# A two-layer decode step: late loads of round two split anew, a maximum in halves, variance, ReLU and outputs moved

## Chip, cores and metric

The kernel runs on one core of a Trainium2 chip. The metric is the device time of one execution in microseconds (us); of several runs the median counts.

## The reference

Four tokens (batch 4, width 640) pass through attention, an MLP, attention again and the MLP again, with the same weights and the same caches in both rounds. All data are float32.

```python
x = x + A(layernorm(x), k_cache, v_cache, wq, wo)   # 32 heads of 128; the last 1024 cache rows
x = x + B(layernorm(x), w1, w2)                     # relu(x @ w1) @ w2, hidden width 1728
x = x + A(layernorm(x), k_cache, v_cache, wq, wo)
x = x + B(layernorm(x), w1, w2)
```

In `A`, q = x @ wq, then for each batch and head softmax(q k^T / sqrt(128)) over 1024 positions, times v, then all heads @ wo. `layernorm` has no gain or bias.

## The kernel before

**Data.** Each head is one record `rec` of 9472 float32 columns on 128 partitions (4736 KB): 640 columns of wq, 4096 of keys (`K`), 4096 of values (`V`), 640 of wo (`WO`). The MLP weights `wm` are 17280 columns. A `store` in SBUF holds five records and the first `FIRST` = 2176 columns of head 0; `ring` (4320 columns) takes MLP weights and parts of records, `kept` (2688) the end of head 26.

**Loads.** All loads stand in one list, `items`, in a fixed order, and are issued by SP in that order. `pump()` issues the next one as soon as no live columns overlap its place; `done(key, lo, hi)` frees columns after the instructions that read them and calls `pump()`. So a load waits for the last reader of its place, and all loads behind it wait too. A semaphore makes SP wait on the chip for that reader.

**Order of heads.** Round one takes heads 0 to 31, round two 27 to 31 and then 0 to 26 (`order`). Heads 27 to 31 are still in the store from round one and are not loaded again, nor are the first 2176 columns of head 0 and the end of head 26. While heads 27 to 31 are computed in round two, what they leave is filled with heads 1 to 5, piece by piece: `places` lists free stretches of the store in the order of use, `run` cuts the stream of records to them at the columns of `CUTS`. `old[i]` is the place of the i-th of the heads 27 to 31. Part of head 31 is parked in PSUM (`park`, copied back by `unpark`) so that MLP weights have room in the place called `spare`.

**One head.** `query`: wq times x (10 matmuls), scaled by VectorE into `qT`. `scores`: 16 matmuls into one of two PSUM tiles `sc_ps` (128 x 1024). `softmax`: maximum on VectorE, exp on ScalarE. `weights`: transpose in 32 x 32 blocks on VectorE and scaling. `values`: 16 matmuls into `o_ps`. `picks`: mask and reduction on VectorE. `output_T`: a matmul that transposes, copied by ScalarE to `oTs`. `project`: wo, 8 matmuls added into `acc`, which holds x. The scores of the next head are issued ahead of the values of this one.

**Start of a round and MLP.** `center` takes the mean off; `deviation` computes the variance (a matmul by ones into a few columns of `acc`, small VectorE steps, a square root on ScalarE). For attention it stands behind the first half of the first head's scores; the first head's query stays unscaled, and its scores are scaled in the exponential. In `mlp` it stands behind the first of five blocks of w1. Then ReLU with the scale on ScalarE (two activations and a copy of 16 columns), transposes on VectorE into `hT`, and 54 tiles of w2.

**Fillers.** `busy` issues matmuls whose result is not used. Every engine executes its instructions in the order in which they are written (`InOrder`, so that most profile lines name line 102).

## Time and profile before

| | |
|---|---|
| median of 3 runs | 713.27 us (712.83 to 715.55) |
| profiled execution | 714.82 us |
| its span | 713.0 us |
| granted TensorE clock | 0.818 |
| TensorE busy (matmuls) | 496.7 us, 70% of the span |
| VectorE busy | 317.3 us, 45% |
| ScalarE busy | 102.2 us, 14% |
| data moved by DMA | 301.98 MB, mean 424 GB/s |

PE is TensorE's matmuls, PEld its weight loads, DVE VectorE, ACT ScalarE, SPq the queue of SyncE on which the loads are issued. A row of the windows view gives a stretch of the span, its length, for each engine busy time and instructions, then the granted TensorE clock, the busy share of the DMA engines and GB/s. A row of the timeline gives start, duration, engine, source line, operation and tiles; in brackets is the idle time before it and what ended it. In the chain of waits each piece has start, duration, engine and tile. Round one ends and round two begins at about 386 us.

### The profile page before, as it was taken

Reading aid. Unit: us, or ns where it says so; the run is one execution under the profiler, and the core shown is the slowest. Engines: PE = TensorE matmul, PEld = TensorE weight load, DVE = VectorE, ACT = ScalarE, POOL = GpSimd, SP = SyncE. Lnnn points to the kernel's source line nnn. Section 1 sums busy time; section 2 is a strip of 40 time slices with the busy share of each in tenths; the row PEclk is TensorE's granted clock in tenths of the full one; section 3 lists DMA queues with packets and bytes.
Section 4 is the critical chain, followed back from the end, with each engine's and each line's share of the span. In section 5 each row is a group of like instructions: output and inputs, shape, how many; then the busy total and the mean of one; then the engine's idle time right before and its main releaser. Section 6 shows DMA issues by size and latency. Waiting matters only on the chain.

```text
span 713.0 us, 8685 instructions
## 1 busy us (share of the span) xinstructions
PE 496.7 (70%) x3722; PEld 202.1 (28%) x3722; DVE 317.3 (45%) x647; ACT 102.2 (14%) x218; POOL 1.1 (0%) x9
## 2 busy tenths in 40 slices
PE   0685684678577468869868899655584676675986
PEld 0321231232232223333314333221231232223322
DVE  2252362353453353546631866525262353363650
ACT  0110110011010110111221321101010011020210
POOL 0000000000000000000000000000000000000000
PEclk9986797677686776877999999979597688797998
DMA  9999999999999999999999999999999999999995
GB/s 396 438 415 449 434 415 445 445 412 442 448 410 442 444 420 425 422 444 421 422 405 409 410 432 424 428 453 432 420 440 435 430 433 425 440 424 422 431 422 237
DMA packets 12598, 301.98 MB, mean 424 GB/s; under 512 B 1408, under 2 KB 1552, under 8 KB 4624
## 3 DMA queue, kind: packets, MB, share of 16 engines
q1 hardware_dynamic: 12528, 301.42, 98.6%
q8 instruction: 29, 0.48, 0.2%
q14 instruction: 9, 0.07, 0.0%
q10 hardware_dynamic: 32, 0.01, 0.0%
HBM read 301.34 MB, written 0.08 MB: 423 GB/s over the span
## 4 chain that ended last, share of the span: by engine, by line
DMA 74%; PE 20%; DVE 3%; another core or an unknown queue 1%; issue 1%; ACT 1%; SPq 0%; ACTq 0%; DVEq 0%
DMA store<-rec 67%; PE sc_ps L102 7%; PE o_ps L102 6%; DMA store<-wm 4%; PE acc L102 3%; PE misc L102 3%; DMA ring<-wm 3%; DVE scratch L102 1%; DVE o_ps L102 1%; ACT oTs L102 1%; DVE small L102 0%; DVE store L102 0%; ACT sc_ps L102 0%; DVE sc_ps L102 0%
## 5 line engine op out<-in xcount | busy, mean ns | idle before, releaser
L102 PE MATMUL sc_ps<-store,qT 128*4 128x512 f32 x1024 | 184.6, 812 | 40.3 <-DMA store<-rec 38.4
L102 PE MATMUL misc<-xT,store 128*128 128x4 f32 x620 | 95.0, 280 | 103.9 <-DMA store<-rec 103.6
L102 PE MATMUL o_ps<-store,scratch 128*16 128x512 f32 x954 | 144.4, 683 | 3.1 <-DVE scratch L102 1.9
L102 DVE TENSOR_REDUCE small<-sc_ps 128x1 f32<-128x1024 f32 x64 | 78.4, 1225 | 148.3 <-PE sc_ps L102 148.3
L102 PEld LDWEIGHTS misc<-xT,store 128*128 128x128 f32 x620 | 89.5, 225 | 161.2 <-DMA store<-rec 125.4
L102 ACT ACTIVATE sc_ps<-sc_ps,small 128x1024 f32<-128x1024 f32 (+1 forms) x68 | 71.5, 1051 | 328.8 <-DVE small L102 316.4
L102 DVE STREAM_TRANSPOSE sc_ps<-sc_ps 128x1024 f32<-128x1024 f32 (+1 forms) x70 | 81.7, 1167 | 0.1
L102 DVE TENSOR_TENSOR o_ps<-o_ps,of_block 128x512 f32<-128x512 f32 x62 | 43.3, 699 | 51.3 <-PE o_ps L102 46.0
L102 PEld LDWEIGHTS sc_ps<-store,qT 128*4 128x4 f32 x1024 | 31.9, 104 | 120.2 <-issue 62.7
L102 PEld LDWEIGHTS o_ps<-store,scratch 128*16 128x16 f32 x954 | 32.8, 113 | 112.8 <-issue 96.8
L102 DVE TENSOR_TENSOR qT<-misc,rows 128x4 f32<-128x4 f32 x61 | 9.5, 156 | 116.0 <-PE misc L102 116.0
L102 PE MATMUL acc<-store,oTs 128*4 128x160 f32 x488 | 34.1, 362 | 18.1 <-ACT oTs L102 17.3
L102 DVE TENSOR_REDUCE scratch<-o_ps 128x128 f32<-128x512 f32 x62 | 42.9, 691 | 2.1
L102 ACT COPY oTs<-o_ps 128x4 f32<-128x4 f32 x62 | 10.1, 162 | 218.0 <-PE o_ps L102 218.0
L102 PE MATMUL o_ps<-rows,scratch 128*128 128x4 f32 x124 | 26.3, 282 | 13.1 <-DVE scratch L102 13.1
L102 PEld LDWEIGHTS o_ps<-rows,scratch 128*128 128x128 f32 x124 | 22.0, 222 | 20.6 <-DVE scratch L102 16.8
L102 DVE TENSOR_TENSOR scratch<-sc_ps,mrt 128x128 f32<-128x128 f32 (+1 forms) x70 | 19.6, 280 | 3.1 <-PE o_ps L102 0.5
L99 PE MATMUL acc<-scratch,ring 128*128 128x160 f32 x2 | 0.9, 539 | 22.3 <-DMA scratch<-xf 22.3
L102 DVE TENSOR_SCALAR mrt<-of_batch,small 128x4 f32<-128x4 f32 x64 | 14.7, 229 | 2.2
L102 PE MATMUL acc<-kept,small 128*1 128x328 f32 (+1 forms) x44 | 14.8, 448 | 0.0
L102 PEld LDWEIGHTS acc<-store,oTs 128*4 128x4 f32 x488 | 6.8, 84 | 24.3 <-ACT oTs L102 22.2
L102 DVE STREAM_TRANSPOSE scratch<-small 128x32 f32<-128x32 f32 x64 | 12.9, 201 | 1.4 <-ACT sc_ps L102 1.4
(83 smaller groups left out, 128.1 us busy)
## 6 DMA issues: line engine op xcount, KB each, us to landing
store<-rec SPq DMA_DIRECT2D x14, 7872.0 KB, 28.3
store<-rec SPq DMA_DIRECT2D x7, 7936.0 KB, 29.6
store<-rec SPq DMA_DIRECT2D x5, 7104.0 KB, 21.4
store<-rec SPq DMA_DIRECT2D x9, 2368.0 KB, 36.1
store<-rec SPq DMA_DIRECT2D x3, 4736.0 KB
store<-rec SPq DMA_DIRECT2D x2, 4416.0 KB, 29.0
store<-rec SPq DMA_DIRECT2D x5, 1024.0 KB, 18.6
store<-rec SPq DMA_DIRECT2D x2, 2304.0 KB, 15.8
```

The source lines that it names most:

```text
L99: r = build(*args, **kwargs)
L102: r = build(*args, **kwargs)
```

## The change

1. `places`: the entry for the wo columns of head 27 is dropped; the last long stretch ends at `FROM` of the place of head 31; then come the first 2176 columns of the store (head 0's, free in round two behind its first scores), the rest of head 31's place, and the ring. Round one no longer frees head 0's first 2176 columns.
2. `deviation` moves from behind the first half of the first scores to behind the first query, together with the load of the table for exp. Its result goes to a bank of `sc_ps` instead of columns of `acc`. In the MLP it gives the deviation by column (`rrow`).
3. The first head's maximum is taken in halves: the first behind the first half of the scores, the second behind the second; they are joined in one step with the scale.
4. In the MLP, transposes come first, and ReLU and scale follow as one VectorE instruction on the transposed block, twice.
5. `output_T` inside the loop writes to `t_ps` instead of `o_ps`, but for the first head of round two, where `t_ps` still holds parked data.
6. Fillers: 344 columns wide instead of 328; in the first MLP at the ends of loads instead of at the ends of blocks; in round two's first heads at other places.

```diff
     places = [("store", old[i] + lo, old[j] + hi) for i, lo, j, hi in (
         (0, 0, 0, K), (0, K + 1024, 0, K + VH), (0, K + VH + 1536, 0, V), (1, 0, 1, K), (1, K, 1, K + VH), (1, K + VH, 1, V),
-        (0, V, 0, WO), (0, WO, 0, REC), (2, 0, 2, V), (1, V, 1, REC), (3, 0, 3, V), (2, V, 2, REC), (3, V, 4, REC))] + [("ring", 0, RING)]
+        (0, V, 0, WO), (2, 0, 2, V), (1, V, 1, REC), (3, 0, 3, V), (2, V, 2, REC), (3, V, 4, FROM))]
+    places += [("store", 0, FIRST), ("store", old[4] + FROM, old[4] + REC), ("ring", 0, RING)]
...
+        if key == ("rec", 0, 0):
+            lo = max(lo, FIRST)
...
-    h_ps, front, warm = sc_ps[0][:, :512], sc_ps[0][:, 512:736], sc_ps[0][:, 768:]
+    h_ps, warm, var = sc_ps[0][:, :512], sc_ps[0][:, 512:768], sc_ps[0][:, 768:768 + B]
...
-    def busy(n=328, to=spare_cols, groups=1):
+    def busy(n=344, to=spare_cols, groups=1):
...
-    def deviation(rows, bias, scale):
-
-        var = variances.pop()
-        pe.matmul(var, ones.to_broadcast([P, P]), squares, start=False, stop=True, skip_group_check=True)
-        dve.tensor_tensor(mrt, var, rows, op=OP.mult)
-        dve.tensor_reduce(sums, mrt, op=OP.add, axis=AX.X)
-        act.activation(rstd, sums, AF.Sqrt, bias=bias, scale=scale / D)
-        if rows is of_batch:
-            dve.tensor_copy(rrow, var)
-            act.activation(rrow, rrow, AF.Sqrt, bias=bias, scale=scale / D)
+
+    def deviation(bias, scale, by_row):
+
+        pe.matmul(var, ones.to_broadcast([P, P]), squares, start=True, stop=True)
+        if by_row:
+            dve.tensor_tensor(mrt, var, of_batch, op=OP.mult)
+            dve.tensor_reduce(sums, mrt, op=OP.add, axis=AX.X)
+        dve.tensor_copy(rrow, var)
+        if by_row:
+            act.activation(rstd, sums, AF.Sqrt, bias=bias, scale=scale / D)
+        act.activation(rrow, rrow, AF.Sqrt, bias=bias, scale=scale / D)
...
             if first and i == 0:
                 if r:
                     unpark(0)
-                deviation(of_batch, eps_dh, float(DH))
-                if r:
                     unpark(1)
-                act.activation(unused, eps, AF.Exp)
+                dve.tensor_reduce(sums, sc_ps[s][:, :512], op=OP.max, axis=AX.X, negate=True)
...
-        dve.tensor_reduce(nmax, sc_ps[s], op=OP.max, axis=AX.X, negate=True)
         if first:
+            dve.tensor_reduce(nmax, sc_ps[s][:, 512:], op=OP.max, axis=AX.X, negate=True)
             dve.reciprocal(rstd, rstd)
-            dve.tensor_tensor(nmax, nmax, rstd, op=OP.mult)
+            dve.scalar_tensor_tensor(nmax, nmax, sums, rstd, op0=OP.min, op1=OP.mult)
             dve.reciprocal(rrow, rrow)
+        else:
+            dve.tensor_reduce(nmax, sc_ps[s], op=OP.max, axis=AX.X, negate=True)
...
-    def output_T(i, last=False):
-        pe.matmul(outs[last][:, :B], on[last], pick, start=True, stop=True)
-        act.copy(oTs[:, i], outs[last][:, :B])
+    def output_T(i, last=False, to=None):
+        to = outs[last][:, :B] if to is None else to
+        pe.matmul(to, on[last], pick, start=True, stop=True)
+        act.copy(oTs[:, i], to)
...
+                if not r and FF < k * FF + FQ * (j + 1) in [hi for _, hi, _, _ in MLP_RING]:
+                    busy()
             done(("w", r), k * FF, k * FF + FF)
             if k == 0:
-                deviation(pick, eps, 1.0)
-                dve.reciprocal(rstd, rstd)
-            elif k < KB - 1 and not r:
-                busy()
-        act.activation(front, h_ps[:, :224], AF.Relu, scale=rstd)
-        act.activation(h_ps[:, 224:FQ], h_ps[:, 224:FQ], AF.Relu, scale=rstd)
-        act.copy(h_ps[:, 464:480], h_ps[:, 416:FQ])
+                deviation(eps, 1.0, False)
+                dve.reciprocal(rrow, rrow)
         busy()
         busy(256)
-        dve.transpose(scratch[:, :224], front)
-        dve.transpose(scratch[:, 224:], h_ps[:, 224:480])
+        for lo, hi in ((0, 224), (224, 480)):
+            if lo:
+                dve.tensor_copy(h_ps[:, 464:480], h_ps[:, 416:FQ])
+            dve.transpose(scratch[:, lo:hi], h_ps[:, lo:hi])
+            h = hT[:, lo // 32:hi // 32, :B]
+            dve.scalar_tensor_tensor(h, h, 0.0, rrow.unsqueeze(1).to_broadcast([P, (hi - lo) // 32, B]),
+                                     op0=OP.max, op1=OP.mult)
...
         center(2 * r)
         query(r, hs[0], 0, True)
-        if r:
-            busy(256, warm, 2)
+        deviation(eps_dh, float(DH), True)
+        act.activation(unused, eps, AF.Exp)
         scores(r, hs[0], 0, True)
         softmax(0, True)
         query(r, hs[1], 1)
+        if r:
+            busy(328, sc_ps[1], 2)
...
             scores(r, hs[n + 1], s)
+            if r and not n:
+                busy(groups=2)
             softmax(s)
...
-            output_T(max(i, 0))
+            output_T(max(i, 0), to=None if r and not n else t_ps[:, :B])
```

More of the change, by code (lines that the diff above doesn't have):

```diff
@@ L336, in unpark @@
                                    (V + 1024, V + 1536, "store", b + K + VH), (V + 1536, REC, "store", c + V + 1536)]
-    h_ps, front, warm = sc_ps[0][:, :512], sc_ps[0][:, 512:736], sc_ps[0][:, 768:]
+    h_ps, warm, var = sc_ps[0][:, :512], sc_ps[0][:, 512:768], sc_ps[0][:, 768:768 + B]
     pad = h_ps[:, 432:464]
     mean = h_ps[:, :B]
-    spare_cols = acc[:, FD:488]
-    variances = [acc[:, 488 + B * i:488 + B * i + B] for i in range(4)]
-    def busy(n=328, to=spare_cols, groups=1):
+    spare_cols = acc[:, FD:504]
+    def busy(n=344, to=spare_cols, groups=1):
         for g in range(groups):
```

## The prediction

> **What bounds the kernel now.** I read the page first, for the engine that is never idle, then windows of the span for the data rate, then, for the stretches where that rate falls, the transfer queue, the chain of waits and the timeline.
>
> ```profile
> GB/s 396 438 415 449 434 415 445 445 412 442 448 410 442 444 420 425 422 444 421 422 405 409 410 432 424 428 453 432 420 440 435 430 433 425 440 424 422 431 422 237
> q1 hardware_dynamic: 12528, 301.42, 98.6%
> 6.00:340.00 334.00, 229.26 (x1510) 91.12 (x1514) 138.22 (x275) 41.53 (x90) 0.00 (x0) 0.78 1.00 432
> 355.00:368.00 13.00, 9.72 (x100) 3.01 (x100) 6.97 (x19) 5.30 (x9) 0.00 (x0) 1.00 1.03 421
> 368.00:373.00 5.00, 2.83 (x23) 0.83 (x25) 0.48 (x3) 0.29 (x1) 0.00 (x0) 1.00 0.97 368
> 375.00:382.00 7.00, 5.07 (x76) 2.25 (x71) 0.75 (x2) 0.99 (x3) 0.00 (x0) 1.00 1.02 388
> 388.00:395.00 7.00, 6.15 (x57) 3.09 (x56) 4.14 (x15) 4.28 (x8) 0.00 (x0) 1.00 1.00 411
> 395.00:398.00 3.00, 2.29 (x24) 0.26 (x16) 2.86 (x7) 0.04 (x1) 0.00 (x0) 1.00 0.97 357
> 398.00:422.00 24.00, 22.42 (x204) 9.96 (x204) 17.76 (x36) 5.96 (x13) 0.00 (x0) 0.94 1.01 430
> 432.00:700.00 268.00, 183.96 (x1390) 75.57 (x1390) 123.87 (x247) 37.06 (x82) 0.00 (x0) 0.82 1.00 430
> 705.49 4.49 PE acc L102 x68
> ```
>
> The input queue moves 301.42 MB. The last column of the windows is the data rate, the one before it the share of the 16 DMA engines in use. At 432 GB/s the bytes alone take 698 us of the 713.0 us span, and for 334 us on one side of the middle and 268 us on the other the rate is 432 and 430. So no engine's arithmetic counts except where it makes the queue run dry, and at the very end, where 68 matmuls of the last MLP follow a landing at 705.49. All that can be won lies between the rounds. Against 432 GB/s the windows lose: 355 to 368, 13 x (1 - 421/432) = 0.33 us; 368 to 373, 0.74; 375 to 382, 0.71; 388 to 395, 0.34; 395 to 398, 0.52. Behind 398 the rate looks whole again, but packets of the larger transfers are counted where they start, so a short hole there doesn't show in a window. It shows when one counts what the queue still holds, by the bytes that start after an instant:
>
> ```profile
> q1 hardware_dynamic: 6587, 139.17, 97.6%
> q1 hardware_dynamic: 5452, 133.10, 97.5%
> q1 hardware_dynamic: 4852, 129.76, 97.4%
> q1 hardware_dynamic: 4071, 119.27, 97.2%
> 427.13 0.50 PE acc L102 x8
> 427.64 21.44 DMA store<-rec
> 413.66 0.33 SPq L102 DMA_DIRECT2D store<-rec  x1
> store<-rec SPq DMA_DIRECT2D x1, 2368.0 KB, 16.7
> ```
>
> These are the queue rows from 379.8, 394.8, 402.9 and 427.6 us to the end. The lists in the code say which transfers were not yet issued. At 427.64: 9216 KB that complete heads 4 and 5, 98,112 KB of heads 6 to 26, 8640 KB of MLP weights and the 80 KB result, 118.83 MB. At the earlier instants, with what lies between: 138.61, 132.53 and 128.20 MB. The difference is what the queue still held: 0.56, 0.57, 1.56 and 0.44 MB, or 1.3, 1.3, 3.6 and 1.0 us of supply at 432 GB/s. With 3.6 us no hole follows (430 GB/s from 398 to 422). With 1.3 us one does, at 375 to 382 and at 395 to 398. So 427.64, where SP at last may issue 7104 KB because the output product of head 31 has read its weights, must be a hole as well. Its size: the transfer before it was issued at 413.66 and landed 16.7 us later, at 430.36; the 7104 KB landed at 427.64 + 21.44 = 449.08. That is 18.72 us for 7.27 MB, which take 16.84 us at full rate, so at most 1.9 us is lost; the page's 25th slice (424 for 17.8 us) gives at least 0.3 us. A landing also carries the spread of 16 engines, the slice loses to lumps, so I take a value between, 0.9 us.
>
> **The change part by part: the places.** Up to the load behind the first scores of head 30 the old list issues 256 + 2304 + 2176 + 2304 = 7040 KB and the new one 2304 + 2368 + 2368 = 7040 KB, at the same events but for the 256 KB, which had come earlier (behind the output product of head 27) and is now part of a later one; supply there was 3.6 us, so 0.6 us less (0.26 MB) is harmless. Then 7104 + 2112 KB become 4160 + 896 + 2816 + 1344 KB. The 4160 KB need only what head 30 leaves, and so go out behind head 30's output product; the 896 KB go where the first 2176 columns of head 0 stood, behind its first scores; the 2816 KB still wait for head 31's product, the 1344 KB for head 0's values.
>
> ```profile
> 419.34 0.71 PE acc L102 x8
> ```
>
> That product ends at 420.05, 7.6 us ahead of 427.64. At 427.64 the queue then holds 0.44 + 5056 KB (5.18 MB) = 5.6 MB, 13 us of supply. The hole closes: 0.9 us gained (0.3 to 1.9). SP issues in order, so the 2816, the 1344 and everything after wait behind the 896 KB; their place is free once head 0's first scores are done, which PE computes ahead of head 31's product, so nothing is held up. There is one transfer more in all. Cost in rows: nothing, while the queue is full.
>
> The Trainium skill, "DMA: Bandwidth & Descriptors", section "Anatomy of one DMA", gives a fixed 2.0 us for each transfer besides its bytes (measured on the other, software path). If queued transfers paid that one after another, the one more would cost 2.0 us and the sum of all parts would be a loss of 0.6 us; the 87 transfers of this kernel would take 174 us beyond their bytes, against 15 us that the span has, so the trace disagrees.
>
> **ReLU behind the transposes.** Rows of the first MLP:
>
> ```profile
> 377.42 0.86 ACT L102 ACTIVATE sc_ps<-sc_ps,small 128x224 f32<-128x224 f32 x2 [8.73 <-PE sc_ps L102]
> 378.31 0.16 ACT L102 COPY sc_ps<-sc_ps 128x16 f32<-128x16 f32 x1
> 378.50 0.75 DVE L102 STREAM_TRANSPOSE scratch<-sc_ps 128x224 f32<-128x224 f32 x2 [9.62 <-ACT sc_ps L102]
> 378.98 0.73 PE L102 MATMUL acc<-ring,scratch 128*4 128x160 f32 x16 [1.33 <-DVE scratch L102]
> 365.86 0.18 DVE L102 SCALAR_TENSOR_TENSOR xT<-sc_ps,xT 128x20 f32<-128x20 f32 x1 [0.22 <-PE sc_ps L102]
> 379.76 0.33 SPq L102 DMA_DIRECT2D ring<-wm  x1
> ```
>
> From the last matmul of the first layer to the first of the second it takes 378.98 - 377.42 = 1.56 us: two activations and a copy of 1.05 us on ACT, then a transpose. After: a transpose (half of 0.75) and one fused max and multiply on 28 columns (0.18, like the row on 20), with 0.1 us of hand-over: 0.7 us. The copy, second transpose and second product lie under the first 28 tiles' matmuls (16 take 0.73, so 56 take 2.6 us). Gain 0.8 us on the issue at 379.76 and the five behind it. The variance matmul in its own bank and the moved fillers lie in waits for weights (PE is busy for 2.83 of the 5 us from 368 to 373, row above) and cost nothing; uncovered, a filler costs up to 0.6 us. Supply at that issue rises from 1.3 to 2.1 us. Of the 0.71 us lost from 375 to 382 a part (the dip ahead of 379) hangs on an earlier issue that does not move; I take 0.2 us gained, bounds 0 and 0.71. The second MLP's hidden layer is ready 0.8 us earlier too, but its end hangs on the landing at 705.49, so nothing.
>
> **Round two's first head.**
>
> ```profile
> 390.25 0.39 PE L102 MATMUL acc<-small 128*128 128x4 f32 x2
> 390.35 0.58 ACT L102 COPY store<-sc_ps 128x512 f32<-128x512 f32 x1 [11.87 <-PE sc_ps L102]
> 391.04 0.69 DVE L102 COPY store<-sc_ps 128x512 f32<-128x512 f32 x1
> 391.53 1.28 PE L102 MATMUL acc<-xT,store 128*128 128x4 f32 x10
> 391.56 1.28 ACT L102 ACT_TABLE_LOAD   x1
> 391.67 1.23 DVE L102 TENSOR_REDUCE small<-sc_ps 128x1 f32<-128x1024 f32 x1
> 393.35 0.16 DVE L102 TENSOR_TENSOR qT<-acc,rows 128x4 f32<-128x4 f32 x1
> 393.66 1.90 PE L102 MATMUL sc_ps<-store,qT 128*4 128x512 f32 x16 [0.85 <-DVE qT L102]
> 399.48 0.60 PE L102 MATMUL sc_ps<-kept,small 128*1 128x256 f32 x4
> ```
>
> Before, DVE does the variance, then the copy at 391.04, then a maximum of 1.23 us, and qT of the next head follows at 393.35. After, the variance matmul (0.39) takes the place of the fillers ahead of the scores, so DVE is free for its copy when the first scores end, 390.35; then a half maximum under the second scores, the other behind them, and the same small steps: qT some 0.5 us earlier, at about 392.9, which is where the query's matmuls (391.53 + 1.28 = 392.81) allow it. New in the way: a filler of some 0.6 us (as at 399.48) stands ahead of the next scores, and on ACT the table load (1.28) now comes before the copy that frees the next scores' buffer. That copy then ends near 392.4, ahead of qT, and is covered; the filler costs 0.25. Uncovered, each would set the scores later by its own length. So these scores start 0.3 us earlier by themselves and 0.8 from the MLP, less what the fuller queue had delayed: about 0.9 us. The transfer issued behind them (at 394.8) finds 1.3 + 0.9 - 0.2 = 2.0 us of supply. Of 0.34 + 0.52 us I take 0.3 gained (0 to 0.86; below nothing, if the filler and the copy are both uncovered, -0.6).
>
> The outputs' own bank changes neither lengths nor the order of a head's steps: the copy of the output (0.16, ahead of each product) stays, at nothing. Filler of 344 for 328 columns: in idle time.
>
> **Sum.** 0.9 + 0.2 + 0.3 = 1.4 us less, all of it by the input ending earlier; the tail from 705.49 on keeps its length. The profiled execution took 714.82 us with a span of 713.0; it becomes 713.4 with 711.6. It stands 1.55 us above the median of the three runs shown, 713.27, from which the change is subtracted: 711.9 us. Half a per cent, 3.6 us, is about what a measurement of this kernel can tell from no change (its own runs lie 0.38% apart).
>
> **The rivals.** *All holes close*: 1.9 + 0.71 + 0.86 = 3.5 us, 709.8. For it: the landing times. Against: the queue at 379 and 395 would still be short. 0.13. *Nothing is gained*: the holes fall on engines that are ahead, and the slowest of the 16 sets the end; 713.3. For it: the last landings stretch over several us. Against: the 7104 KB landed late as a whole, on its slowest engine. 0.14. *A fixed price for each transfer* (the rule named above, here as a pause at the one more): 0.6 us slower, 713.9; 0.02. *The buffer copy and the filler decide*: if ACT's copy ends after 393.7, the hole at 395 grows by 0.6 us, and with nothing at 379, 0.9 - 0.6 leaves 713.0; 0.06. *The clock falls*, the one that ends slower:
>
> ```profile
> 80.00:90.00 10.00, 9.69 (x60) 4.35 (x59) 4.05 (x9) 1.37 (x3) 0.00 (x0) 0.60 0.98 425
> 357.00:400.00 43.00, 32.63 (x344) 13.36 (x342) 16.76 (x48) 10.11 (x20) 0.00 (x0) 1.00 1.01 402
> ```
>
> Between the rounds PE has the full clock (1.00) for 43 us, and elsewhere 0.60. The change moves the fillers that stand there. At 0.60, the part of PE's 32.63 us that waits for no landing, by estimate 13 us, takes 8.7 us longer; 2 us of supply cover little of it, and some 6 us become holes: 713.3 + 6 - 1.4 = about 718. It decides if the granted clock from 370 to 400 falls under 0.85, where 13 us become 15.3, more than the supply. Against: fillers are added as well as taken, and no idle stretch grows. 0.05.
>
> **How the numbers follow.** Forecast 0.59, rivals 0.13, 0.14, 0.02, 0.06 and 0.05, and 0.01 for a loss that I have not seen. The range goes from the first rival with a little less than its whole, 710.0, to 714.4, which takes in no gain (713.3) and a second hole grown by the bounds of its costs (0.6 + 0.5 of a lost head start). Faster by over 0.5% (under 709.7): half of the first rival, 0.06. Slower (over 716.8): the clock and the unseen, 0.06. Within: 0.88.
>
> **What would show it.** Right: the queue's content at the time of head 31's output product is over 5 MB; 4160 KB issued near 419; the rate from 395 to 398 over 390 GB/s, from 375 to 382 over 395; the first second-layer matmul of the first MLP 0.7 us behind the last of the first; the next scores of round two some 0.9 us earlier; the same 4.5 us behind the last landing but one. Wrong: a clock under 0.85 between 370 and 400, or a landing order in which the end does not follow the holes.

## The result, and the profile after

| | before | changed |
|---|---|---|
| median of the runs | 713.89 us (712.80 to 716.24) | 718.93 us (717.47 to 719.66) |
| ratio, 95% interval | 1 | 1.0065 (1.0044 to 1.0087) |
| profiled execution, span | 714.82, 713.0 us | 718.88, 717.2 us |

The change costs 0.65%, some 4.6 us; the prediction was 711.9 us (710.0 to 714.4), so it was wrong in sign and outside its range. Here and below a ratio and its interval are computed from all runs of both kernels, not from the two medians shown, and can differ from their quotient by about 0.1%.

The page of the changed kernel: the data rate in 40 slices, and the input queue (packets, MB, share of 16 engines).

```profile
GB/s 394 446 409 436 450 430 422 439 441 422 431 442 429 431 435 426 418 442 421 424 399 390 259 431 430 450 431 433 438 435 429 434 439 427 437 424 419 432 425 293
q1 hardware_dynamic: 12672, 301.42, 98.3%
```

The same bytes were moved, and there is one deep dip: the 23rd slice moved 259 GB/s where the kernel before had 410. The windows of the changed kernel (busy times of PE, PEld, DVE, ACT and POOL; then granted clock, DMA share, GB/s) place it:

```profile
6.00:340.00 334.00, 223.03 (x1518) 91.25 (x1518) 139.30 (x277) 42.38 (x91) 0.00 (x0) 0.80 1.00 431
355.00:368.00 13.00, 11.47 (x100) 3.65 (x100) 7.60 (x20) 5.42 (x9) 0.00 (x0) 0.83 1.02 418
368.00:373.00 5.00, 3.42 (x24) 0.92 (x26) 0.34 (x2) 0.30 (x1) 0.00 (x0) 1.00 0.99 372
375.00:382.00 7.00, 5.99 (x79) 2.33 (x73) 1.34 (x5) 0.00 (x0) 0.00 (x0) 1.00 1.02 385
388.00:395.00 7.00, 4.23 (x28) 1.64 (x28) 2.38 (x9) 2.56 (x5) 0.00 (x0) 0.66 0.97 373
395.00:398.00 3.00, 3.00 (x17) 1.85 (x9) 1.06 (x4) 0.58 (x1) 0.00 (x0) 0.50 0.45 142
398.00:422.00 24.00, 23.19 (x191) 9.45 (x194) 17.49 (x37) 5.78 (x13) 0.00 (x0) 0.88 0.88 342
432.00:700.00 268.00, 196.30 (x1400) 80.08 (x1400) 127.25 (x248) 36.37 (x83) 0.00 (x0) 0.76 1.00 432
370.00:400.00 30.00, 23.12 (x213) 9.47 (x213) 6.69 (x24) 4.32 (x8) 0.00 (x0) 0.84 0.90 342
```

Outside 388 to 422 the rate did not move (431 for 432 on one side, 432 for 430 on the other). Inside, 395 to 398 fell from 357 to 142 GB/s and 398 to 422 from 430 to 342. Against 432 GB/s that is 7 x (1 - 373/432) = 1.0 us, 2.0 us and 24 x (1 - 342/432) = 5.0 us, 8.0 in all, where the kernel before lost 0.34 + 0.52 + 0.1. (Packets count where they start, so these are not yet microseconds of the span; the last landing, below, is 5.76 us late.) The granted clock from 395 to 398 is 0.50; the half clock lasts from 390.2 to 403.85. In the timeline of the changed kernel (start, duration; in brackets the idle time before and what ended it) one sees why:

```profile
390.46 1.89 PE L102 MATMUL sc_ps<-store,qT 128*4 128x512 f32 x8 [0.52 <-DVE rows L102]
...
390.86 1.28 ACT L102 ACT_TABLE_LOAD   x1
...
392.37 0.58 ACT L102 COPY store<-sc_ps 128x512 f32<-128x512 f32 x1
392.98 0.69 DVE L102 COPY store<-sc_ps 128x512 f32<-128x512 f32 x1 [2.58 <-ACT store L102]
393.59 0.68 DVE L102 TENSOR_REDUCE small<-sc_ps 128x1 f32<-128x512 f32 x1
394.33 1.89 PE L102 MATMUL sc_ps<-store,qT 128*4 128x512 f32 x8 [1.98 <-DVE small L102]
396.15 2.30 PE L102 MATMUL acc<-xT,store 128*128 128x4 f32 x10
...
398.71 1.02 PE L102 MATMUL sc_ps<-store,qT 128*4 128x512 f32 x2
...
399.42 3.62 PE L102 MATMUL sc_ps<-store,qT 128*4 128x512 f32 x14
```

The two halves of the same scores in the kernel before:

```profile
389.20 1.12 PE L102 MATMUL sc_ps<-store,qT 128*4 128x512 f32 x8
390.56 1.04 PE L102 MATMUL sc_ps<-store,qT 128*4 128x512 f32 x8
```

In the changed kernel the second half of round two's first scores does not follow the first. TensorE waits 1.98 us for the half maximum: three steps in a row, ScalarE's copy, VectorE's copy, the reduction (0.58 + 0.69 + 0.68). The wait stands in the program: the matmuls write the other 512 columns, but of the PSUM tile that the reduction reads. The row of the first scores shows the same once more: they wait 0.52 us for VectorE's copy of the variance (`rows`), which the change put into other columns of this tile. No run puts the halves into two tiles, so that it is the tile is read from the code and from these two waits. And all matmuls run at half clock: eight of them in 1.89 us, the query in 2.30 instead of 1.28, the next head's sixteen until 403.04. Before, those sixteen ended at 393.66 + 1.90 = 395.56. They are 7.48 us late, and that splits so: the first scores start 1.26 us later (390.46 for 389.20; 0.79 of it because the last weights of the first MLP landed later, most of the rest is the wait for the variance), the wait is 1.98, and the rest, 4.24 us, is what the slower matmuls and the filler among them add, less the pauses that stood there before.

The next transfers go out behind the first eight of those sixteen. SP's issue in the kernel before:

```profile
394.76 0.33 SPq L102 DMA_DIRECT2D store<-rec  x1
```

and in the changed kernel:

```profile
401.41 0.33 SPq L102 DMA_DIRECT2D store<-rec  x1
```

The end of the changed kernel's chain of waits (start, length, what the chain runs through):

```profile
711.25 2.83 PE acc L102 x68
```

The issue is 6.65 us late, and the last landing, 711.25 for 705.49, 5.76 us: the difference, 0.9 us, is near the 1.3 us of supply that the prediction counted in the queue. The span grew by only 4.2 us because the 68 matmuls at the very end took 2.83 us in this profile and 4.49 in the one before, where the granted clock over them was 0.58 (705.5 to 710) and here 1.00 (711 to 714).

### The profile page after: what moved, and what is told of

It reads as the page before. It is cut to its first block, busy times and chain, and to the rows that moved or that the text cites. A ratio compares the mean times of both kernels' runs of the same rounds, so it can differ in the third digit from the quotient of the medians.

```text
span 717.2 us, 8637 instructions
## 1 busy us (share of the span) xinstructions
PE 508.3 (71%) x3728; PEld 206.1 (29%) x3728; DVE 318.5 (44%) x653; ACT 100.2 (14%) x212; POOL 1.1 (0%) x9
## 4 chain that ended last, share of the span: by engine, by line
DMA 69%; PE 25%; DVE 3%; another core or an unknown queue 1%; issue 1%; ACT 1%; SPq 0%; ACTq 0%
DMA store<-rec 61%; PE sc_ps L102 10%; PE o_ps L102 7%; DMA store<-wm 4%; PE misc L102 4%; PE acc L102 3%; DMA ring<-wm 3%; PE t_ps L102 1%; DVE scratch L102 1%; DVE o_ps L102 1%; ACT oTs L102 1%; DVE small L102 0%; ACT store L102 0%; DVE rows L102 0%
## 5 line engine op out<-in xcount | busy, mean ns | idle before, releaser
L102 PE MATMUL sc_ps<-store,qT 128*4 128x512 f32 x1024 | 189.1, 828 | 43.7 <-DMA store<-rec 39.0
L102 PE MATMUL misc<-xT,store 128*128 128x4 f32 x620 | 97.4, 284 | 98.0 <-DMA store<-rec 97.6
L102 PE MATMUL o_ps<-store,scratch 128*16 128x512 f32 x960 | 150.6, 703 | 2.0 <-DMA store<-rec 1.5
L102 DVE TENSOR_REDUCE small<-sc_ps 128x1 f32<-128x1024 f32 (+1 forms) x66 | 78.7, 1192 | 154.8 <-PE sc_ps L102 154.8
L102 PEld LDWEIGHTS misc<-xT,store 128*128 128x128 f32 x620 | 91.9, 231 | 157.2 <-DMA store<-rec 121.4
L102 ACT ACTIVATE sc_ps<-sc_ps,small 128x1024 f32<-128x1024 f32 x64 | 69.8, 1091 | 325.9 <-DVE small L102 317.5
L102 ACT COPY oTs<-t_ps 128x4 f32<-128x4 f32 x59 | 9.6, 162 | 211.2 <-PE t_ps L102 211.2
L102 PE MATMUL t_ps<-rows,scratch 128*128 128x4 f32 x118 | 25.7, 288 | 11.0 <-DVE scratch L102 10.3
L102 PEld LDWEIGHTS t_ps<-rows,scratch 128*128 128x128 f32 x118 | 21.8, 230 | 17.2 <-DVE scratch L102 13.1
L102 PE MATMUL acc<-kept,small 128*1 128x344 f32 (+1 forms) x50 | 17.3, 481 | 0.0
## 6 DMA issues: line engine op xcount, KB each, us to landing
store<-rec SPq DMA_DIRECT2D x1, 4160.0 KB, 20.7
```

The source lines that it names most:

```text
L102: r = build(*args, **kwargs)
```

## The experiments

Two theories stood at first. **The wait** (W in the expectations): the half maximum holds the second scores back, and everything behind them. **The clock** (G): TensorE does too little between 383 and 390 us and is cut to half clock at 390.2, wait or no wait. What each run did to the chain is read from one number of its profile, the end of the next head's scores (395.56 before, 403.04 changed).

**The maximum whole again**, all else of the change kept:

```
-                dve.tensor_reduce(sums, sc_ps[s][:, :512], op=OP.max, ...)
...
-            dve.tensor_reduce(nmax, sc_ps[s][:, 512:], op=OP.max, ...)
+            dve.tensor_reduce(nmax, sc_ps[s], op=OP.max, ...)
```

> The changed kernel with the first head's maximum taken whole again, behind both halves of the scores; all else as changed. Theory W (the wait): the second half of the first scores waits for the half maximum, which stands behind the table load and two copies; without it these matmuls follow the first half at once, the scores' start of the next head comes 3 us or more earlier, the hole from 395 to 406 us mostly closes, and the time is 714 us or less. Theory G (the clock): TensorE had already been cut to half clock at 390.2 us, ahead of that wait, by too little work from 383 to 390 us; without the half maximum it still is, for 10 us or more, and the time stays over 716 us.

Measured: 714.56 us against 714.09, ratio 0.9998 (0.9979 to 1.0017). Its timeline:

```profile
390.40 3.56 PE L102 MATMUL sc_ps<-store,qT 128*4 128x512 f32 x16 [0.51 <-DVE rows L102]
...
395.94 1.90 PE L102 MATMUL sc_ps<-store,qT 128*4 128x512 f32 x16
```

and the end of its chain of waits:

```profile
706.82 2.80 PE acc L102 x68
```

Sixteen matmuls in one run without a wait; the next scores end at 397.84. One window of half clock is still there (390.39 to 393.8; the clock changes in windows of 3.41 us), not four. So the halves are the whole 0.65% within the intervals, and the rest of the change nets to nothing (0.2% at most).

**The first half maximum issued behind the second scores**, so that there are two halves and no wait:

```
-                dve.tensor_reduce(sums, sc_ps[s][:, :512], op=OP.max, ...)    (in scores)
+            dve.tensor_reduce(sums, sc_ps[s][:, :512], op=OP.max, ...)        (in softmax)
             dve.tensor_reduce(nmax, sc_ps[s][:, 512:], op=OP.max, ...)
```

> The changed kernel with both half maxima kept as two instructions, but the first one issued behind the second half's scores too. Theory W (the wait of the second half's scores on the first half maximum is the cost): as without the halves, 714 to 715 us, since no matmul waits for it any more. Rival D (the two half maxima themselves, on VectorE, cost the time): nothing changes, about 718.5 us.

Measured: 715.27 against 713.76, ratio 1.0012 (0.9995 to 1.0029); the sixteen matmuls run through again (390.13, 3.45 us). Two reductions are not what costs (0.12%, an interval that holds 1); the place between the scores is.

**The halves alone** in the kernel before (variance and table load where they were):

```
                 act.activation(unused, eps, AF.Exp)
+                dve.tensor_reduce(sums, sc_ps[s][:, :512], op=OP.max, ...)
```

> The kernel before with the maximum in halves alone, the first half behind the copies as in the change; variance, places, ReLU, fillers and outputs as before. Theory W: this one edit is enough; the second half's scores start 2 to 3 us later than before, and the kernel is 3 to 5 us slower than before, 717 to 719 us. Rival J (it takes the table load ahead of the copies, which came with the moved variance, to make the wait long): under 1.5 us slower.

Measured: 715.59, ratio 1.0029 (1.0010 to 1.0048), 2.1 us. In its timeline:

```profile
392.16 1.04 PE L102 MATMUL sc_ps<-store,qT 128*4 128x512 f32 x8 [1.75 <-DVE small L102]
393.13 1.91 PE L102 MATMUL acc<-xT,store 128*128 128x4 f32 x10
395.39 3.59 PE L102 MATMUL sc_ps<-store,qT 128*4 128x512 f32 x16 [0.35 <-DVE qT L102]
```

The wait is 1.75 us, nearly as long as in the changed kernel, but at full clock; the clock falls only afterwards, for two windows (393.58 to 400.41). It is under half of the loss, between the two expectations.

**The wait made longer**: the changed kernel, the half maximum of round two taken three times.

```
-                dve.tensor_reduce(sums, sc_ps[s][:, :512], op=OP.max, ...)
+                for _ in range(3 if r else 1):
+                    dve.tensor_reduce(sums, sc_ps[s][:, :512], op=OP.max, ...)
```

> The changed kernel with the first half maximum of round two taken three times over instead of once (the same value; two more reductions of 0.68 us on VectorE while TensorE waits). The wait theory: the second half of the scores starts 1.36 us later (about 395.7) and the time grows by 1.2 to 2 us, to 720.1 to 720.9. If the loss is bounded elsewhere (transfers that the next head awaits land late anyhow, or the clock window sets the end): no change, 718.9.

Measured: 720.32 against 714.23, ratio 1.0086 (1.0062 to 1.0111), 1.4 us over the changed kernel's 718.93 for 1.45 us more of idle time in its timeline:

```profile
397.54 1.89 PE L102 MATMUL sc_ps<-store,qT 128*4 128x512 f32 x8 [3.43 <-DVE small L102]
```

By these point values each microsecond of wait costs one. The intervals of the two kernels overlap (1.0044 to 1.0087 and 1.0062 to 1.0111), but the profiles agree: the last landing comes 3.16 us later (714.41 for 711.25), 1.76 of which the first scores were late already (392.22 for 390.46). The loss is not bounded by a landing elsewhere.

**The table load behind the copies**, in the changed kernel:

```
-        act.activation(unused, eps, AF.Exp)      (round two: ahead of the first scores)
...
                     unpark(0)
                     unpark(1)
+                    act.activation(unused, eps, AF.Exp)
```

> The changed kernel, halves of the maximum kept, but in round two the load of the exponential's table is issued behind the two copies from PSUM instead of ahead of them. The wait theory: ScalarE's copy starts 0.8 to 1.2 us earlier, so the first half maximum and the second half of the scores do (about 393.2 instead of 394.3), and the time falls by 0.8 to 1.5 us, to 717.4 to 718.1. If the length of the wait did not matter beyond its being there (the clock's halving decides): 718.9, no change.

Measured: 718.75, ratio 1.0056 (1.0038 to 1.0074); no difference from the changed kernel that can be told, as the second theory had it, but for another reason, as its timeline shows:

```profile
391.86 0.59 ACT L102 COPY store<-sc_ps 128x512 f32<-128x512 f32 x1 [1.45 <-PE sc_ps L102]
...
393.82 1.89 PE L102 MATMUL sc_ps<-store,qT 128*4 128x512 f32 x8 [1.96 <-DVE small L102]
```

The copy waits for the first scores, which at half clock end at 391.86, and from there the same three steps make the same wait, 1.96. I had taken the table load for the longest piece of it; at half clock it lies under the scores.

**The clock held by fillers.** First five fillers between the halves, one behind the query and three more in the first MLP; then the same with two between the halves.

```
                     unpark(0)
                     unpark(1)
+                    for _ in range(5):      (2 in the second run)
+                        busy()
```

> The changed kernel with more fillers in round two's first head and ahead of it: three more in the wait for the last w2 tiles of the first MLP, one behind the first query, five between the two halves of the first scores; the half maximum and its wait stay. Theory G: the granted clock stays 1.00 from 383 to 404 us, and the time falls to 714 us or less. Theory W: the second half of the scores still starts at about 394.3 us, the hole from 395 on shrinks only by the shorter matmuls behind it (some 2 us of 6), and the time is about 716 us.

> As the run with the clock held, but with two fillers instead of five between the halves of the first scores, so that they end before the half maximum does. If the wait alone sets the time: within 1 us of the changed kernel, 718 to 719. If the long stretch at half clock (13.6 us in the changed kernel) has a share of its own and the fillers shorten it: 716 to 717.5.

Measured: 718.21, ratio 1.0052 (1.0031 to 1.0072), and 717.51, 1.0049 (1.0034 to 1.0064). Half clock lasted 3.4 and 6.8 us instead of 13.6, yet little came back. Both runs moved something else as well: with the filler behind the query the first scores came 0.7 and 1.2 us later, and five fillers ran 0.96 us past the half maximum. The next scores ended at 401.11 and 401.13, so the gain in clock was partly spent on the way. Hence the cleaner run, **two fillers in the wait and nothing else**:

```
                     unpark(0)
                     unpark(1)
+                    busy()
+                    busy()
```

> The changed kernel with two fillers of 344 columns between the halves of round two's first scores and nothing else: they lie inside TensorE's wait for the half maximum. If the long stretch of half clock (390.2 to 403.85 us in the changed kernel's profile) comes from the wait's idle time: the clock is back within two windows (by about 397), the next head's scores take 1.9 to 2.1 us instead of 4.3 and end at 400.2 to 401.2 instead of 403.04, and as every microsecond there has so far cost nearly one at the last landing, the time is 1.5 to 2.7 us less: 716.2 to 717.4. If the wait alone makes the loss: 718.9, no change; if the fillers push the second half back: more.

Measured: 716.37 against 714.00, ratio 1.0026 (1.0015 to 1.0037), so 2.6 us less than the changed kernel. TensorE in its timeline:

```profile
393.62 1.87 PE L102 MATMUL acc<-kept,small 128*1 128x344 f32 x4
395.82 1.04 PE L102 MATMUL sc_ps<-store,qT 128*4 128x512 f32 x8 [0.33 <-DVE small L102]
396.79 1.28 PE L102 MATMUL acc<-xT,store 128*128 128x4 f32 x10
...
398.36 2.07 PE L102 MATMUL sc_ps<-store,qT 128*4 128x512 f32 x16
```

The end of its chain:

```profile
709.52 2.80 PE acc L102 x68
```

The clock is back after one window (391.31 to 394.72), the second half takes 1.04 us again, the next scores end at 400.43 although in this profile the first started 1.49 us later than in the changed kernel's. The second half starts 3.87 us behind the first in both kernels, so the wait is as long as it was, and only the idle time in it is gone: filling it ended the long stretch of half clock. It is not the only thing that makes such a stretch, as the variance alone shows below. What is left, 0.26% or 1.9 us, is about the size of the wait.

**The same fillers with the halves alone**:

> The kernel before with the maximum in halves alone (1.0029 when run without fillers: 715.6 against 713.6), and two fillers of 328 columns in round two's wait between the halves. If the clock that falls behind the wait makes most of those 2 us (16 matmuls of the next scores in 3.59 us instead of 1.90): 0.8 to 1.7 us less, 714.0 to 714.8. If the wait itself makes them: 715.6.

Measured: 715.85, ratio 1.0025 (1.0009 to 1.0041): no gain. Its timeline:

```profile
392.38 1.04 PE L102 MATMUL sc_ps<-store,qT 128*4 128x512 f32 x8
...
395.01 1.90 PE L102 MATMUL sc_ps<-store,qT 128*4 128x512 f32 x16 [0.38 <-DVE qT L102]
```

The end of its chain:

```profile
707.02 4.49 PE acc L102 x68
```

Here the clock never falls, and 1.8 us are lost all the same: the second half starts 1.82 us later than before (392.38 for 390.56) and the last landing comes 1.53 later (707.02 for 705.49). That is the wait's price by itself. That the half clock made most of the loss of the halves alone was wrong.

**The filler taken from the kernel before** (the two 256-column groups behind round two's first query):

```
-        if r:
-            busy(256, warm, 2)
```

> The kernel before without the two filler groups behind the first query of round two, nothing else. Theory G: with less work in that window the clock falls to half near 390 us and the kernel loses 2 to 5 us. Theory W: no wait is added, no change within 0.3 us.

Measured: 715.02, ratio 1.0001 (0.9982 to 1.0019). Taking that filler out costs nothing that shows in the median. This kernel's own profile did show half clock from 392.86 to 403.1, and the profiled run, 717.11, was the slowest of its ten; what the clock did in the other nine is not on record for this stretch.

**The parts that should gain.** The new places alone; the ReLU behind the transposes alone; both; both with the changed kernel's two fillers:

```
-        (0, V, 0, WO), (0, WO, 0, REC), (2, 0, 2, V), ... (3, V, 4, REC))] + [("ring", 0, RING)]
+        (0, V, 0, WO), (2, 0, 2, V), ... (3, V, 4, FROM))]
+    places += [("store", 0, FIRST), ("store", old[4] + FROM, old[4] + REC), ("ring", 0, RING)]
...
-        act.activation(front, h_ps[:, :224], AF.Relu, scale=rstd)
+            dve.transpose(scratch[:, lo:hi], h_ps[:, lo:hi])
+            dve.scalar_tensor_tensor(h, h, 0.0, rrow..., op0=OP.max, op1=OP.mult)
```

> The kernel before with the new places alone. Both theories, as the prediction: the queue no longer runs short at 427.6 us, 0.9 us faster than before (0.3 to 1.9), about 713.

> The kernel before with ReLU and scale behind the transposes alone. The prediction gave 0.2 us. By the traces so far: the first matmul of the second layer comes 0.85 us earlier, but from its third load on the layer waits for landings, so its end does not move, and the time stays within 0.5 us of before.

> The kernel before with the two parts of the change that closed a hole or did no harm: the late places of round two split anew, and the ReLU behind the transposes; the maximum whole, variance and table load where they were. The sum of the prediction for these two was -1.1 us: 712.8 against 713.9. What the parts alone have shown (0.0 and -0.6 us, each with an interval of about 1 us) allows 712.6 to 714.4. If the gains are eaten wherever a window of half clock falls into 388 to 406 us: 713.9, no difference.

> The kernel before with the late places split anew, the ReLU behind the transposes, and the two fillers of the changed kernel (behind the second query, behind the next head's scores); the maximum whole, variance where it was. If windows of half clock over 394 to 400 us take back part of what the two edits gain (the profile of the two without fillers lost 1.4 us at 398 to 406): 0.5 to 1.0 us faster than those two, 712.8 to 713.2 against 714.2 for the kernel before. If the fillers only stand in the way of TensorE: 713.6 to 714.3.

Measured: 714.45, ratio 1.0000 (0.9986 to 1.0013); 713.89, 0.9992 (0.9978 to 1.0006); 713.63 against 714.23, 0.9989 (0.9975 to 1.0002); 713.58 against 714.48, 0.9990 (0.9978 to 1.0001). The last two are the best point values of all, 0.7 to 0.8 us under the kernel before, but none is settled: each interval still holds 1. In the profile of the places alone the transfer does what it should (SP's issue in the timeline):

```profile
420.66 0.33 SPq L102 DMA_DIRECT2D store<-rec  x1
```

Its size and the time from issue to landing:

```profile
store<-rec SPq DMA_DIRECT2D x1, 4160.0 KB, 21.6
```

And two windows of the same kernel:

```profile
395.00:398.00 3.00, 3.00 (x16) 0.27 (x12) 2.83 (x8) 0.21 (x1) 0.00 (x0) 0.50 0.92 359
398.00:406.00 8.00, 7.75 (x75) 3.42 (x67) 5.71 (x11) 2.84 (x5) 0.00 (x0) 0.99 0.98 375
```

The 4160 KB landed 21.6 us after their issue, though their bytes take 9.9 us at 432 GB/s, so 11.7 us of other work stood ahead of it: no hole there. The gain went elsewhere in that execution: a window of half clock fell on 394.7 to 398.1, and 398 to 406 moved 375 GB/s instead of 429.

**The variance moved alone** (variance, roots and table load behind the first query, maximum whole), then with the two fillers, then with the table load behind the copies; and the changed kernel with a whole maximum but without the two fillers:

```
-                deviation(of_batch, eps_dh, float(DH))      (in scores)
-                act.activation(unused, eps, AF.Exp)
...
+        deviation(of_batch, eps_dh, float(DH))              (behind the first query)
+        act.activation(unused, eps, AF.Exp)
```

> The kernel before, with one part of the change: the variance of the row, both square roots and the load of the exponential's table are issued behind the first query instead of between the halves of the first scores; the maximum stays whole, the filler stays behind the query. The wait theory (only the second half's wait for the first half maximum costs): within 0.7 us of the kernel before (713.2 to 714.6), the second half of round two's first scores following the first at once. The rival that moving the variance and the table load costs by itself (the copies from PSUM stand behind 2 to 3 us of ScalarE's work, buffers come free later, and what is issued behind them is late): 1.5 us or more over the kernel before (over 715.4), with the losses at 395 to 398 and 398 to 406 above 1.5 us together.

> The kernel before with the variance, the square roots and the table load behind the first query (as in the run of the variance alone, +2.0 us), and with the two fillers of the changed kernel: 2 groups of 328 columns behind the second query and 2 behind the next head's scores. If the clock over the next head's scores is the loss (16 matmuls in 3.59 us at half clock there, 1.90 at full): the fillers keep TensorE busy, and the time comes back to within 0.8 us of the kernel before (713.4 to 715.0). If the table load ahead of ScalarE's copy is the loss: no change against the variance alone, 715.5 to 716.5.

> The kernel before with the variance and both square roots behind the first query, but in round two with the load of the exponential's table behind the two copies from PSUM. If the table load ahead of the copies is the loss: the copies end 1.3 us earlier than with the variance alone, the whole maximum starts when the scores end, and the time is within 0.7 us of the kernel before (713.5 to 714.9). If the clock is the loss: 715.5 to 716.5, and half clock from about 390.5 over the next scores again.

> The changed kernel with the maximum whole (which cost nothing against the kernel before), without its two fillers behind the second query and behind the next head's scores. If the fillers hold the clock: the next scores run at half clock (about 3.6 us for 16 matmuls) and the time grows by 1 to 2 us, to 715.2 to 716.2. If they do nothing: 714.2, as with them.

Measured: 715.96, ratio 1.0028 (1.0012 to 1.0044); 716.20, 1.0029 (1.0015 to 1.0043); 715.34, 1.0013 (0.9998 to 1.0028); 714.61, 0.9998 (0.9983 to 1.0014). So the variance's move costs 2 us on its own, which neither theory had; the fillers that the change brings do nothing measurable, with it or in the changed kernel; moving the table load back may return half, within the noise. In the profile of the variance alone nobody waits for a half, but the clock is cut at 390.49 for three windows:

```profile
392.90 2.30 PE L102 MATMUL acc<-xT,store 128*128 128x4 f32 x10
...
395.55 3.59 PE L102 MATMUL sc_ps<-store,qT 128*4 128x512 f32 x16 [0.35 <-DVE qT L102]
```

And its window just ahead of the cut:

```profile
387.07:390.49 3.42, 2.88 (x30) 1.94 (x30) 1.10 (x7) 0.50 (x3) 0.00 (x0) 1.00 1.01 421
```

The trace shows a second piece that has no half clock in it. ScalarE's copy now stands behind the table load (391.88 for 390.35 before), VectorE's copy behind ScalarE's, and the whole maximum behind that: it starts at 393.08 instead of 391.67 (row in the prediction), 1.4 us late. It is as late at full clock: in the changed kernel with the maximum whole and no fillers, whose clock is full there, the scores end at 392.17 and the maximum starts at 393.28. With the fillers the clock was cut for one window only and the next scores ended 2.13 us earlier, yet the time is the same; so the parts of these 2 us are not separated.

Why the changed kernel with the whole maximum, which holds the same move, is not slower than the kernel before stays open; the gain of places and ReLU (0.8 us by their point value) covers a part of it, the intervals could cover the rest.

**The profiles side by side.** Each row is one profiled execution; a late end of the next scores comes back in the last landing that releases the 68 matmuls. Two runs are not in it, the late table load and the clock held by five fillers: there a later landing releases only the last 8 to 24.

| kernel | ratio | next scores end | last landing |
|---|---|---|---|
| before | 1 | 395.56 | 705.49 |
| places and ReLU, filled | 0.9990 | 396.00 | 705.33 |
| places alone | 1.0000 | 396.62 | 705.58 |
| halves alone, wait filled | 1.0025 | 396.91 | 707.02 |
| variance, filled | 1.0029 | 397.01 | 707.08 |
| places and ReLU | 0.9989 | 397.10 | 706.27 |
| ReLU alone | 0.9992 | 397.19 | 706.39 |
| changed, halves behind | 1.0012 | 397.55 | 706.85 |
| changed, maximum whole | 0.9998 | 397.84 | 706.82 |
| the same, no fillers | 0.9998 | 398.07 | 706.35 |
| halves alone | 1.0029 | 398.98 | 707.48 |
| variance alone | 1.0028 | 399.14 | 707.99 |
| changed, wait filled | 1.0026 | 400.43 | 709.52 |
| variance, table late | 1.0013 | 400.50 | 709.03 |
| before, filler taken out | 1.0001 | 401.11 | 709.57 |
| changed, clock held, 2 fillers | 1.0049 | 401.13 | 710.25 |
| changed | 1.0065 | 403.04 | 711.25 |
| changed, longer wait | 1.0086 | 405.83 | 714.41 |

From the halves alone on, the landing is late by the scores' delay less 0.8 to 1.7 us. That is about the 1.3 us of supply that the prediction counted in the queue at 394.8: what is later than that is lost one for one. (With the halves alone and the wait filled the landing is late by 1.53 us for 1.35, and with the variance and fillers by 1.59 for 1.45, so not every microsecond of that supply is there in every execution.) Ratios follow less strictly: the kernel with the filler taken out has its scores 5.55 us late in its one profile and loses nothing by its median. One profile is one execution, and the clock falls differently from one to the next.

## Why the prediction was wrong

**What bounds the kernel** held, but for the tail (below). Starvation of the queue between the rounds costs the time, the supply at 394.8 is as thin as counted, and the loss is a hole there.

**The places** were right in mechanism. The 4160 KB go out right behind head 30's product. With all the delay ahead of it that product ends at 427.15 in the changed kernel (420.05 before; among the prediction's signs it stands as "near 419"). Its timeline and its issues:

```profile
427.20 0.33 SPq L102 DMA_DIRECT2D store<-rec  x1
```

```profile
store<-rec SPq DMA_DIRECT2D x1, 4160.0 KB, 20.7
```

They landed 20.7 us later and take 9.9 us by themselves, so the queue held 10.8 us of other work where it had held 1.0: the hole is closed. But its size, 0.9 us, could not be confirmed by a time (1.0000, 0.9986 to 1.0013). The one transfer more cost nothing that shows: the new places, with that transfer, are at 1.0000, where 2.0 us more against 0.9 us gained would be 1.0015. The fixed 2.0 us are those of the Trainium skill, "DMA: Bandwidth & Descriptors", section "Anatomy of one DMA", which gives them for one DMA of the other path and not as a price in a full queue.

**ReLU behind the transposes** was right in its first step and wrong in its end. In the changed kernel

```profile
377.43 0.42 DVE L102 STREAM_TRANSPOSE scratch<-sc_ps 128x224 f32<-128x224 f32 x1 [8.71 <-PE sc_ps L102]
...
378.12 0.73 PE L102 MATMUL acc<-ring,scratch 128*4 128x160 f32 x16 [0.44 <-DVE scratch L102]
...
385.76 1.26 PE L102 MATMUL acc<-ring,scratch 128*4 128x160 f32 x30 [1.44 <-DMA ring<-wm]
```

the second layer starts 0.69 us behind the first (0.7 predicted), but 375 to 382 moves 385 GB/s, not over 395, and the last group of weights lets the matmuls go at 385.76, where before it was

```profile
384.97 1.26 PE L102 MATMUL acc<-ring,scratch 128*4 128x160 f32 x30 [0.64 <-DMA ring<-wm]
```

This start moves from one execution to the next (384.74 to 387.52 over the profiles), but in none of them is it ahead of the kernel before by the 0.8 us. The layer ends on landings, so the 0.8 us were not handed on to round two's first head, and the 0.9 us of head start built on them did not come. By time the edit alone is at 0.9992 (0.9978 to 1.0006), for 0.2 us predicted.

**Round two's first head** is the step that failed. "DVE is free for its copy when the first scores end" overlooked that DVE's copy waits for ACT's (2.58 us of idle time in its row, ended by ACT). The prediction had ACT's copy, behind the table load, end "near 392.4" and took it for covered; it ended at 392.95, and the half maximum stood behind both copies. "A half maximum under the second scores" took an overlap for granted that the program does not have: both halves lie in one tile, and the matmuls behind a reader of that tile wait for it. The prediction asked who is queued on ACT and DVE but not who waits for the new reader. The same oversight once more, at some 0.5 us, is the variance in that tile, which holds up the first scores (with the maximum whole too, 0.51 us, so it is no part of the price below). In place of the 0.3 us gained it cost 0.67% (1.0065 less 0.9998), 4.8 us: about 2.0 for the wait (what is left when it is filled, 1.0026, less 0.9998), and 2.8 for the half clock that ends early when the wait is filled (1.0065 less 1.0026).

**The rivals.** The clock was given 718 us, a chance of 0.05 and a threshold: under 0.85 from 370 to 400. The row above says 0.84, and the time was 718.9. That both numbers fit is luck for the most part. Its mechanism was not the one I named: the filler taken out by itself does nothing (1.0001). An idle stretch did grow, which the prediction denied. Its price is also smaller than worked out, 2.8 us instead of 6; the wait, which no rival held, makes up the rest. The buffer copy and the filler, at 0.6 us, were too small by far and not the cause: with the copy ahead of the table load again the kernel is at 1.0056, and with the maximum whole it is at 0.9998 with the fillers and without them.

**The tail** does not keep its length: 4.49 us before, 2.83 in the changed kernel, about 2.8 in most others, 4.49 to 4.75 in three of the experiments' profiles. The granted clock makes the difference: in those four profiles it is at half from 702 or 704 on for 6.8 us, in the others with 68 matmuls at the end it is full there. That adds 1.7 us to a run or not, and is part of the spread of the kernel before (711.8 to 719.8 over its runs).

## What to carry to other kernels

A reduction moved between two groups of matmuls overlaps them only if the program lets the second group go ahead of it; here two halves of one PSUM tile did not count as two buffers, so ask of every moved reader who writes that tile next. Where the queue holds only a microsecond or two of supply, work out how much later the instruction ends behind which the next transfer is issued, and charge all beyond the supply one for one. An idle stretch of two microseconds on TensorE can cost again as much in half clock behind it: filling the wait gave back over half of the changed kernel's loss, though nothing with the halves alone (1.0025 for 1.0029).

## What the runs showed of the hardware

In all profiles here the granted clock changes in steps of 3.41 us (390.2 to 403.85 is four), between 1.0 and 0.5 with nothing between. It was cut without an idle window ahead: in the changed kernel, in the two windows before the cut at 390.2, TensorE was busy for

```profile
383.40:386.80 3.40, 1.96 (x42) 0.94 (x34) 0.00 (x0) 0.00 (x0) 0.00 (x0) 1.00 1.03 422
386.80:390.20 3.40, 2.85 (x30) 1.92 (x20) 1.47 (x8) 0.00 (x0) 0.00 (x0) 1.00 1.01 397
```

1.96 and 2.85 us. The Trainium skill, "TensorE: Matmul & The Clock Gate", section "What's actually happening", has the same step (a free-running window of 3413 ns) and half clock after at least one idle window; the trace agrees on the step and not on the idle window. With the variance alone 2.88 us in the window ahead was cut too (row above), while the kernel before kept the full clock through this stretch (1.00 from 357 to 400, row in the prediction). What decides is not settled, and the cut falls differently from one execution to the next in kernels whose code is the same up to that point: at 390.39 in the changed kernel with the maximum whole, and only at 396.11 in the same kernel without the fillers, which stand later. A comparison of one half per cent needs the medians, not one profile.
